# Planning the next batch's attention apart from its token mixing, with x and u in one buffer

## The chip, the cores and the metric

The kernel runs on one core of a Trainium2 chip. The metric is device time in microseconds (us), the median of the runs of one kernel. The core has TensorE (PE, matrix products into PSUM, a memory of eight banks), VectorE (DVE), ScalarE (ACT), GpSimd (POOL), which here mostly issues loads, and SyncE (SP), which here issues transposes and stores. 16 DMA engines carry out what POOL, SP and ACT issue.

## The reference, cut to what matters

Eight batches of sliding-window attention (8 heads of 64, 576 positions, a window of 128, a linear distance bias), whose output x (576 x 512 per batch) goes through a mixer: token mixing across the positions, then channel mixing, each with a residual.

```
scores = scale * q @ k.T;  masked to 0 <= rel < 128, plus -slope*|rel|
x      = softmax(scores) @ v                      # heads side by side: 576 x 512
h      = relu(x.T @ w_tok1) @ w_tok2              # 576 -> 256 -> 576
u      = x + h.T
out    = u + relu(u @ w_ch1) @ w_ch2              # 512 -> 1536 -> 512
```

## The kernel before, in words

The whole program is straight-line code. `Plan` collects operations (`op`, `dma`), each with an engine, a cost, the buffers it makes, adds to, rewrites or reads, and a **rank**. `Plan.run` then simulates the engines with those costs and at each step starts, on the engine that is free first, the ready operation of the lowest rank; `Plan.emit` writes the instructions in the order so found. On the chip each engine runs its own list strictly in that order, with semaphores for the waits. So costs and ranks only shape the order; a due time that has been given to an operation (`after`) does too, and is no wait on the chip. `NUDGES` is a list of `number:rank shift:due time` for single operations, by their number in the order of creation.

A `Ring` is a set of equal buffers; `plan.buf(name)` takes the first that comes free. `x` of two batches (a pair, 2 x 576 rows as nine blocks of 128, the ninth, `TAIL`, holding 64 rows of each) lies in ring `xb`, which has one buffer, and `u` in ring `ub`, which has two. q and k blocks go through five `qk` slots, v blocks through five `v` slots, transposed q/k through seven `qkT` slots.

Work per batch `b`:

- **Loads**: `load` issues q, k, v of each block on POOL, in one fixed order (pair by pair, blocks 0, 1, 2, 3, 7, TAIL, 4, 5, 6, and in each q, k, v), each waiting for a free slot. A **hold** is a small POOL copy that reads batch `b`'s finished uT at a set place in this order, so everything behind it on POOL waits until that uT is complete. Before, `HOLDS = {4: ("v", 3, 0)}`: ahead of v of pair 3, block 0, POOL waits for batch 4's uT.
- **Attention** (`side`): `transposes` (from pair 1 on by SP's DMA transpose, line 761), `scores` (line 809: products over 64 rows into PSUM banks 0 to 3, `TWO`; line 824: two exponentials on ACT; line 834: masks on DVE), `scores_two` (line 855, two blocks of two pairs at once), `values` (line 897: products with v into one of the four single banks 4 to 7; lines 910, 913 and 919: reciprocal and normalisation into x).
- **Token mixing** (`token_mix`): line 944 x with `W1`, line 954 the tail rows, relu, line 987 with `W2`, line 1005 u = x + product on DVE; then u is transposed into uT, for batches 0 to 2 on PE (line 1022), from batch 3 on by SP's DMA transpose (line 1013).
- **Channel mixing** (`main`): first product by `chunk` (line 1502) or, where `UNITS` says so, by `unit` (line 1402, fewer products and more sums); second product by `second` (line 1679); line 1545 and 1590 for the tail; results evicted on DVE (lines 1650, 1597) and stored.

While `main(b)` runs, `side(b + 1)` is planned beside it, so that PE always has channel products to run between the steps of the attention. What decides their order is the rank. `along(base, length, total)` gives ranks that rise from `base` to `base + length` as the costs add up to `total`. `main(b)` rises over its own length `n`; before, `side(b + 1)`, attention and token mixing in one sequence, rises over `SPREAD * n`, with `SPREAD = 0.38`:

```
side(nb, along(base - 1e5, 1.0, 1.0) if b == 0 else along(base, SPREAD * n, tot))
```

Of the kernel before, what the change touches and what calls it, by code (L numbers as in the profile page):

```python
# [14 lines left out]


SEM = 40.0
SPREAD = 0.38


class Buf:
# [10 lines left out]
    def __call__(self):  # L32
        got = self.ring.slots[self.slot[0]]
        return got if len(self.slot) == 1 else self.ring.pair(self.slot)


class Ring:
# [34 lines left out]
class Plan:  # L72
# [9 lines left out]
    def op(self, eng, cost, emit, rank, makes=(), adds=(), rewrites=(), part=None, uses=(), reads=(), needs=(),  # L82
           after=0.0, order=None, bus=0.0, other=None, mode=0, behind=(), narrow=False):
        def many(x):
            return list(x) if isinstance(x, (list, tuple)) else [x]

        o = Op()
        o.eng, o.cost, o.emit, o.rank, o.after, o.part = eng, cost, emit, rank, after, self.part
        o.t0 = o.done = None
        o.order, o.bus, o.other, o.mode, o.narrow = order, bus, other, mode, narrow  # L90
        o.n = len(self.ops)
        o.deps = set(many(needs))
        o.behind = list(behind)
        o.bufs = []
        for b in many(makes):
            b.writers.append(o)
            o.bufs.append(b)
        for b in many(adds):
            o.deps.update(b.writers)
            b.writers.append(o)  # L100
            o.bufs.append(b)
        for b in many(rewrites):
            o.deps.update(u for u in b.users if u not in b.later)
            b.later.append(o)
            b.writers.append(o)
            o.bufs.append(b)
        if part is not None:
            b, key = part
            b.parts.setdefault(key, []).append(o)
            o.bufs.append(b)  # L110
        for b in many(uses):
            o.deps.update(b.writers)
            o.bufs.append(b)
        for b, key in many(reads):
            o.deps.update(b.parts[key])
            o.bufs.append(b)
        o.deps.discard(o)
        for b in o.bufs:
            b.users.append(o)
        self.ops.append(o)  # L120
        return o
# [204 lines left out]
    def emit(self, spin):  # L326
# [20 lines left out]
        for _, _, go in sorted(work, key=lambda w: w[:2]):  # L347
# [15 lines left out]
FROM_U = 3  # L363
# [22 lines left out]
GROUPS = (((0, 1, 2, 3), 250),)  # L386
UORDER = (1, 5, 2, 6, 3, 7, 4)
UNIT_RANK = 0
NUDGES = ("611:-21079:100923 615:-377:0 618:6245:106227 624:11583:0 628:-3532:0 631:-20512:118175 632:4405:0 "
          "635:13739:113529 638:-6964:114135 641:43614:0 643:-19605:120680 648:13951:125840 652:20901:132489 "  # L390
          "656:1592:130617 662:-3783:94988 668:12595:102360 672:0:99525 676:-4021:0 691:3986:0 694:4455:102094 "
          "706:-16795:109525 710:11799:0 717:5009:114541 723:-30772:115527 725:-13156:0 727:1700:0 731:-799:113884 "
          "737:-15688:124087 742:88:126037 747:-10649:132061 750:-29110.6:133561.55 752:1864:0 753:7662:141715 "
          "756:18322:0 757:13696:0 758:5979:130815 759:2748:0 760:-6228:0 761:25117:132703 763:-2147:0 765:-1777:134943 "
          "766:12861:138150 769:4570:135329 774:-3476:0 778:14785:0 780:7181:136913 782:6347:136777 796:5332:0 799:9009:0 "
          "801:8201:142134 808:2736:0 813:9918:154475 818:-1109:0 820:-5330:154387 833:-4650:0 835:34387:124325 "
          "837:-15506:120235 843:8673:0 857:-16826:126349 858:1715:130121 859:24976:132690 862:8001:133653 "
          "869:22770:125235 870:11407:127731 885:3734:139098 891:9282:135579 895:-4722:0 906:6597:0 929:-1024:0 "
          "934:1522:0 937:4392:0 939:-1560:0 942:20915:0 948:771:175554 950:-4529:179605 951:995:176861 980:-2682:165866 "
          "981:-2735:0 983:1098:0 989:-8428:0 992:-4728:0 995:4194:0 1000:4211:156722 1005:3799:169472 1010:-2057:164371 "  # L400
          "1013:-4825:0 1019:7261:0 1032:-2615:175960 1038:-4243:0 1044:-3493:182549 1047:-1700:185338 1048:8146:185482 "
          "1054:3724:185348 1056:2724:0 1068:-1298:0 1070:3393:0 1074:20899:194114 1077:45251:0 1080:18007:0 "
          "1081:-2386:195024 1087:458:209375 1088:1:199812 1091:-1643:199488 1097:-2044:205608 1111:2214:211061 "
          "1114:17600:0 1119:-16086:212462 1121:-6088:0 1124:52293:0 1133:0:215904 1147:208:186538 1149:1234:0 "
          "1154:3339:0 1163:6504:0 1166:5025:0 1173:-13218:195991 1174:-7990:194582 1175:11221:198039 1181:18370:199015 "
          "1189:-770:198395 1195:5140:0 1201:243:206584 1202:-5634:204124 1213:15048:0 1219:1629:209744 "
          "1232:-23729:221022 1233:-4369:0 1235:2272:0 1237:-12249:0 1238:-11167:221075 1240:4249:0 1241:4209:0 "
          "1242:7504:0 1255:5295:0 1256:0:234956 1257:14642:0 1258:12581:0 1260:3619:0 1262:4895:0 1264:11531:232963 "
          "1267:-4292:227279 1276:5714:238024 1280:962:0 1283:-2021:240378 1288:-141:235787 1290:-9906:246722 "
          "1305:-17082:0 1316:331:0 1318:-36744:224142 1320:-20516:0 1325:23513:0 1328:7362:0 1331:-20168:227572 "  # L410
          "1332:-6676:0 1335:2767:0 1338:-7764:230640 1343:-4826:0 1344:8492:0 1347:6686:0 1361:914:0 1363:6921:0 "
          "1364:10157:0 1367:6998:238996 1368:-7883:243068 1371:-1965:238074 1378:-1479:249284 1382:8303:0 1386:7721:0 "
          "1399:-2853:246581 1401:-6638:250221 1402:-752:252012 1403:-9427:251897 1407:-2824:0 1427:-5105:253889 "
          "1431:-2423:252435 1443:3256:263701 1444:354:262085 1457:-151:263359 ")
UNIT_LATE = False
SECOND_LATE = False
GATE = True
BANKS = 8
ALIKE = 0
PAUSE = 150  # L420
HOLDS = {4: ("v", 3, 0)}
UNITS = [0, 0, 0, 3, 0, 3, 2, 3]
FILL = 60000.0
START = 4300.0
# [27 lines left out]
def kernel(  # L452
# [59 lines left out]
    ring("qkT", QT, [P, 2 * NHP, P])  # L512
    ring("pe", 3, [P, 2, 4, 2, P])
    ring("rt", 4, [P, 2, 4, 1], F32)
    ring("xb", 1, [P, NB, DM])
    ring("ub", 2, [P, NB, DM])
    ring("xt", XT, [P, DM])
    ring("r10", 1, [P, NJ, DM])
    ring("r11", 1, [P, NJ, DM])
# [518 lines left out]

    def opening(rank):

        xb, ub = xbs[0], ubs[0] = plan.buf("xb"), plan.buf("ub")
        r1 = r1s[0] = plan.buf("r10")
        uT = plan.buf("uT")
        uts[0] = (uT, None, list(range(NC)))
# [265 lines left out]
            mix(hp)  # L1310
        wides.append(marks["first"])

    def side(b, rank):
        pr, half = b // 2, b % 2
        if half == 0:
            xbs[pr], ubs[pr] = plan.buf("xb"), plan.buf("ub")
        two = pr in PAIRED
        if half:
            units = [5, 6, 7] + [TAIL] * (pr == 0) + [NC] if two else [4, 5, 6, 7] + [TAIL] * (pr == 0)
        else:  # L1320
            units = [1, 2, 3, TAIL] if pr - 1 in PAIRED else [0, 1, 2, 3, TAIL]
            if pr - 1 in PAIRED:
                values(pr, 0, None, marks["next"], rank, 0)
        prev = None
        for u in units + [None]:
            if u is not None:
                need = [(pr, u)]
                if half and u == 5:
                    need.insert(0, (pr, NC))
                if u == TAIL and pr:  # L1330
                    need.append((pr, 2 * NC - 1))
                if half and u == NC and two:
                    need.append((pr + 1, 0))
                for w in need:
                    if w not in qkT or (u == TAIL and w[1] == TAIL and pr == 0):
                        transposes(*w, rank(0 if by_transfer(*w) else 450))
                hf = half if u == TAIL and pr == 0 else None
                if half and u == NC and two:
                    pb = marks["next"] = scores_two(pr, rank(450))
                else:  # L1340
                    pb = scores(pr, u, hf, rank(450), wides if b == 1 else ())
            if prev is not None:
                values(pr, prev[0], prev[1], prev[2], rank)
            prev = None if u is None else (u, hf, pb)
        token_mix(b, rank)

    def gated(*bufs):
        for x in bufs:
# [368 lines left out]
    for b in range(B):  # L1717
# [5 lines left out]
        if b + 1 < B:  # L1723
            nb = b + 1
            tot = SIDE[min(nb // 2, 1)][nb % 2] + 8 * 216 + 216 + (5 if nb % 2 else 4) * (656 if nb < FROM_U else 432)
            if nb > 1:
                tot -= 450 * sum(by_transfer(nb // 2, x) for x in (ORDER[:6], ORDER[6:])[nb % 2])
            side(nb, along(base - 1e5, 1.0, 1.0) if b == 0 else along(base, SPREAD * n, tot))
            for o in wait:
                o.behind.append(marks["score"])  # L1730
            for x in gates:
                x[0] = marks["score"]
# [39 lines left out]
```

## Time and profile before

| | |
|---|---|
| median of 3 runs | 274.07 us (273.73 to 274.9) |
| span of the profiled execution | 272.2 us |
| median less that span | 1.87 us |
| PE busy | 263.6 us, 97% |
| weight loads busy | 191.8 us, 70% |
| DVE, ACT, POOL busy | 224.7, 150.7, 114.7 us |
| loads' DMA queue | 89.4% of 16 engines' span |
| instructions | 7391 |

The page gives the profiled execution's time as its span, from the first to the last instruction; the runs' times also hold what lies around the span. Rows of the views name the line, the engine, the operation and `out<-in` by the program's tile names, with x and a count; in brackets or behind a bar stands the idle time ahead of an instruction and what ended it.

### The profile page before, as it was taken

Reading aid. Unit: us, or ns where it says so; the run is one execution under the profiler, and the core shown is the slowest. Engines: PE = TensorE matmul, PEld = TensorE weight load, DVE = VectorE, ACT = ScalarE, POOL = GpSimd, SP = SyncE. Lnnn points to the kernel's source line nnn. Section 1 sums busy time; section 2 is a strip of 40 time slices with the busy share of each in tenths; the row PEclk is TensorE's granted clock in tenths of the full one; section 3 lists DMA queues with packets and bytes.
Section 4 is the critical chain, followed back from the end, with each engine's and each line's share of the span. In section 5 each row is a group of like instructions: output and inputs, shape, how many; then the busy total and the mean of one; then the engine's idle time right before and its main releaser. Section 6 shows DMA issues by size and latency. Waiting matters only on the chain.

```text
span 272.2 us, 7391 instructions
## 1 busy us (share of the span) xinstructions
PE 263.6 (97%) x2965; PEld 191.8 (70%) x2992; DVE 224.7 (83%) x520; ACT 150.7 (55%) x267; POOL 114.7 (42%) x147
## 2 busy tenths in 40 slices
PE   7989999999999999999999999999999999999994
PEld 5767566676686655587786756498886758589883
DVE  7887699978897569688999478698998989976983
ACT  6973796226881298107992089308973089506700
POOL 8978796840397007800870307800651050004000
PEclk9999999999999999999999999999999999999999
DMA  8999999999999979999999999999999580035005
GB/s 201 178 173 180 167 148 183 157 156 175 186 127 161 192 162 78 137 119 210 200 149 119 142 228 96 140 154 142 212 132 67 110 239 2 2 82 171 4 10 183
DMA packets 160338, 38.59 MB, mean 142 GB/s; under 512 B 146544, under 2 KB 159472, under 8 KB 160304
## 3 DMA queue, kind: packets, MB, share of 16 engines
q0 software_dynamic: 109968, 19.64, 89.4%
q1 hardware_dynamic: 49104, 17.70, 33.4%
q10 hardware_dynamic: 1232, 0.79, 1.0%
q8 instruction: 23, 0.38, 0.5%
q14 instruction: 11, 0.09, 0.1%
HBM read 35.85 MB, written 9.44 MB: 166 GB/s over the span
## 4 chain that ended last, share of the span: by engine, by line
PE 90%; DMA 3%; POOL 3%; issue 1%; ACT 1%; DVE 0%; POOLq 0%
PE ps L1679 27%; PE ps L1502 15%; PE ps L1402 12%; PE ps L897 6%; PE ps L809 5%; PE ps L987 4%; PE ps L944 4%; PE ps L1545 4%; PE ps L1590 4%; DMA W<-in_moe_w_tok_dram 2%; POOL v L623 1%; DMA qkT<-qk 1%; POOL qk L630 1%; PE ps L772 1%; PE ps L1488 1%
## 5 line engine op out<-in xcount | busy, mean ns | idle before, releaser
L614 POOL DMA_DIRECT2D v<-in_v_dram x36 | 30.5, 849 | 76.4 <-PE ps L897 72.8
L824 ACT ACTIVATE pe<-ps 128x1024 bf16<-128x1024 f32 (+1 forms) x56 | 51.3, 969 | 3.1 <-PE ps L809 3.0
L1502 PE MATMUL ps<-uT,WC 128*128 128x512 bf16 x182 | 46.0, 379 | 0.7 <-issue 0.2
L1508 ACT ACTIVATE r<-ps 128x512 bf16<-128x512 f32 x45 | 26.4, 601 | 35.9 <-PE ps L1502 33.8
L1679 PEld LDWEIGHTS <-r 128*128 128x128 bf16 x384 | 36.8, 98 | 7.4 <-issue 0.7
L1679 PEld LDWEIGHTS <-s 128*128 128x128 bf16 x288 | 27.8, 98 | 5.8 <-DVE s L1527 0.4
L614 POOL DMA_DIRECT2D qk<-in_k_dram x35 | 30.3, 873 | 3.7 <-DMA qk<-in_k_dram 1.6
L834 DVE TENSOR_TENSOR pe<-pe,mask 128x1024 bf16<-128x1024 bf16 (+1 forms) x48 | 30.5, 650 | 1.6 <-ACT pe L824 1.4
L614 POOL DMA_DIRECT2D qk<-in_q_dram x35 | 30.2, 867 | 3.7 <-DMA qkT<-qk 1.7
L1502 PEld LDWEIGHTS <-WC 128*128 128x128 bf16 x196 | 17.7, 98 | 18.1 <-issue 0.5
L1417 ACT COPY raw<-ps 128x512 f32<-128x512 f32 x27 | 15.5, 597 | 22.6 <-PE ps L1402 22.6
L1679 PE MATMUL ps<-WC,r 128*128 128x256 bf16 x192 | 24.9, 273 | 0.0
L1679 PE MATMUL ps<-WT,s 128*128 128x256 bf16 x192 | 24.7, 273 | 0.0
L1679 PE MATMUL ps<-WT,r 128*128 128x256 bf16 x192 | 23.8, 273 | 0.1
L897 PEld LDWEIGHTS <-pe 128*128 128x128 bf16 (+1 forms) x480 | 19.5, 99 | 5.6 <-DVE pe L834 0.8
L1426 DVE TENSOR_TENSOR r<-ps,raw 128x512 bf16<-128x512 f32 x30 | 20.2, 680 | 3.3 <-ACT raw L1417 2.8
L897 PE MATMUL ps<-v,pe 128*128 128x65 bf16 (+1 forms) x480 | 22.8, 194 | 0.1
L1005 DVE TENSOR_TENSOR ub<-ps,xb 128x512 bf16<-128x512 f32 x32 | 20.5, 683 | 2.7 <-ACT r L1508 0.9
L913 DVE TENSOR_TENSOR xb<-ps,rt 128x256 bf16<-128x256 f32 (+1 forms) x52 | 21.4, 417 | 0.5
L1650 DVE TENSOR_TENSOR raw<-ps,ub 128x512 f32<-128x512 f32 x25 | 17.0, 686 | 5.8 <-PE ps L1679 5.8
L1402 PE MATMUL ps<-tt,WS 128*128 128x256 bf16 x132 | 18.8, 273 | 0.1
L809 PEld LDWEIGHTS <-qkT 64*128 64x128 bf16 x448 | 11.9, 94 | 8.3 <-issue 5.9
(143 smaller groups left out, 479.4 us busy)
## 6 DMA issues: line engine op xcount, KB each, us to landing
out_dram<-raw SPq DMA_DIRECT2D x19, 256.0 KB, 4.4
qk<-in_q_dram POOLq DMA_DIRECT2D x30, 128.0 KB, 5.4
qk<-in_k_dram POOLq DMA_DIRECT2D x30, 128.0 KB, 5.4
v<-in_v_dram POOLq DMA_DIRECT2D x28, 128.0 KB, 5.1
WC<-in_moe_w_ch_dram POOLq DMA_DIRECT2D x8, 384.0 KB, 7.5
out_dram<-raw POOLq DMA_DIRECT2D x6, 256.0 KB, 3.4
out_dram<-ob SPq DMA_DIRECT2D x5, 256.0 KB, 4.1
v<-in_v_dram POOLq DMA_DIRECT2D x16, 64.0 KB, 4.8
```

The lines of the kernel that those rows point to most:

```text
L614: nc.gpsimd.dma_start(out=to()[p0 : p0 + n, :, :], in_=rows(src, b, s0, n))
L809: pe_.matmul(wide(e)[:, i, kind, a:z], lhsT=ts[kb]()[e * D : (e + 1) * D, NHP + i, :], rhs=ts[blk]()[e * D : (e + 1) * D, i, a:z], start=T ...
L824: act_.activation(out=pb()[:, e, :, lo:, c0:c1_], in_=wide(e)[:, :, lo:, c0:c1_], func=ACT.Exp, scale=scale)
L834: dve_.tensor_tensor(out=o, in0=o, in1=heads(mk, es), op=ALU.mult)
L897: pe_.matmul(view()[a:z, at, i, :], lhsT=pb()[:, e, i, kind, a:z], rhs=vb()[:, h, 0 : D + 1], start=m == 0, stop=m == len(mms) - 1, skip_g ...
L913: dve_.tensor_tensor(out=x4(), in0=view()[r0:r1_, :, :, 0:D], in1=rt()[r0:r1_, 0:n, :, :].broadcast_to([r1_ - r0, n, 4, D]), op=ALU.mult)
L1005: plan.op("DVE", 690, lambda blk=blk, ht=ht, hs=hs: dve_.tensor_tensor(out=ub()[:, blk, :], in0=ht()[:, hs], in1=xb()[:, blk, :], op=ALU.a ...
L1402: pe_.matmul(bk()[:, c * HS : (c + 1) * HS], lhsT=l(c, cb), rhs=r(cb), start=new and c == 0 and cb == 0, stop=cb == 1, skip_group_check=True)
L1426: add = plan.op("DVE", 690, lambda: dve_.tensor_tensor(out=o(), in0=half_of(bk), in1=half_of(e), op=ALU.add), rk + UNIT_RANK, uses=[bk, e] ...
L1502: pe_.matmul(ct()[:, :], lhsT=WC1[:, cb, t * P : (t + 1) * P], rhs=uT()[:, cb, :], start=cb == 0, stop=cb == NCB - 1)
L1508: plan.op("ACT", 600, lambda t=t, ct=ct: act_.activation(out=r2()[:, t, :], in_=ct()[:, :], func=ACT.Relu), rk, part=(r2, t), uses=[ct], o ...
L1679: pe_.matmul(bk()[:, c * HN : (c + 1) * HN], lhsT=l(t, c), rhs=w(t), start=first, stop=g == 1 and t == HK - 1, skip_group_check=True)
```

## The change

- Ring `xb` (one buffer) and ring `ub` (two) become one ring `xu` of three. A pair takes one buffer; u is written over x. `View` gives u its own list of writers and parts on x's buffer.
- `side` takes two ranks: one for attention, one for token mixing. Attention's ranks of batch `b + 1` go from `base - 0.2 n` to `base + 0.2 n`, those of its token mixing from `base + 0.2 n` to `base + 0.35 n`. For batch 1 both stay as they were.
- The holds become `{2: ("k", 2, 0), 4: ("k", 3, 8)}`: a new one ahead of k of pair 2, block 0, waits for batch 2's uT; that for batch 4 moves from ahead of v of pair 3, block 0, to ahead of k of pair 3, block 8 (TAIL).
- Another list of `NUDGES`: 145 entries in place of 178. It reaches back to operation 155; that of before begins at 611.

```diff
-SPREAD = 0.38
+SCORE = (-0.2, 0.4)
+TOKEN = (0.2, 0.15)
...
+class View:
+    def __init__(self, buf):
+        self.buf, self.writers, self.parts, self.later = buf, [], {}, []
+
+    def __call__(self):
+        return self.buf()
...
-            o.bufs.append(b)
+            o.bufs.append(getattr(b, "buf", b))
...
-NUDGES = ("611:-21079:100923 615:-377:0 618:6245:106227 624:11583:0 628:-3532:0 631:-20512:118175 632:4405:0 "
...
+NUDGES = ("155:0:56492 156:63405:0 160:24808:0 297:-72622:0 300:0:37910 316:0:47700 323:0:46277 326:0:53492 "
...
-HOLDS = {4: ("v", 3, 0)}
+HOLDS = {2: ("k", 2, 0), 4: ("k", 3, 8)}
...
-    ring("xb", 1, [P, NB, DM])
-    ring("ub", 2, [P, NB, DM])
+    ring("xu", 3, [P, NB, DM])
...
-        xb, ub = xbs[0], ubs[0] = plan.buf("xb"), plan.buf("ub")
+        xb = xbs[0] = plan.buf("xu")
+        ub = ubs[0] = View(xb)
...
-    def side(b, rank):
+    def side(b, rank, rank2):
         pr, half = b // 2, b % 2
         if half == 0:
-            xbs[pr], ubs[pr] = plan.buf("xb"), plan.buf("ub")
+            xbs[pr] = plan.buf("xu")
+            ubs[pr] = View(xbs[pr])
...
-        token_mix(b, rank)
+        token_mix(b, rank2)
...
-            side(nb, along(base - 1e5, 1.0, 1.0) if b == 0 else along(base, SPREAD * n, tot))
+            mixt = 8 * 216 + 216 + (5 if nb % 2 else 4) * (656 if nb < FROM_U else 432)
+            if b == 0:
+                near = along(base - 1e5, 1.0, 1.0)
+                side(nb, near, near)
+            else:
+                side(nb, along(base + SCORE[0] * n, SCORE[1] * n, tot - mixt), along(base + TOKEN[0] * n, TOKEN[1] * n, mixt))
```

More of the change, by code (lines that the diff above doesn't have):

```diff
@@ L100, in op @@
             b.writers.append(o)
-            o.bufs.append(b)
+            o.bufs.append(getattr(b, "buf", b))
         for b in many(rewrites):
@@ L105, in op @@
             b.writers.append(o)
-            o.bufs.append(b)
+            o.bufs.append(getattr(b, "buf", b))
         if part is not None:
@@ L109, in op @@
             b.parts.setdefault(key, []).append(o)
-            o.bufs.append(b)
+            o.bufs.append(getattr(b, "buf", b))
         for b in many(uses):
             o.deps.update(b.writers)
-            o.bufs.append(b)
+            o.bufs.append(getattr(b, "buf", b))
         for b, key in many(reads):
             o.deps.update(b.parts[key])
-            o.bufs.append(b)
+            o.bufs.append(getattr(b, "buf", b))
         o.deps.discard(o)
@@ L388 @@
 UNIT_RANK = 0
-NUDGES = ("611:-21079:100923 615:-377:0 618:6245:106227 624:11583:0 628:-3532:0 631:-20512:118175 632:4405:0 "
[L390 to L414, printed above, removed]
```

19 rows, old and new, of the table NUDGES are left out of this document.

## The prediction

> **What bounds the kernel now.** I read the page first (span, busy shares, chain), then the busy time by stretch, what TensorE waited for, and the timelines around the places that the change touches.
>
> ```profile
> span 272.2 us, 7391 instructions
> PE 263.6 (97%) x2965; PEld 191.8 (70%) x2992; DVE 224.7 (83%) x520; ACT 150.7 (55%) x267; POOL 114.7 (42%) x147
> PE 90%; DMA 3%; POOL 3%; issue 1%; ACT 1%; DVE 0%; POOLq 0%
> ```
>
> TensorE (PE) is busy 263.6 of 272.2 us and makes 90% of the chain that ended last. Everything else only matters where it makes PE wait. The next view tells where PE is idle; its columns are the stretch, its length, and busy us with instruction counts for PE, weight loads, VectorE, ScalarE, GpSimd, then the granted clock.
>
> ```profile
> 0.00:20.00 20.00, 17.30 (x295) 12.95 (x295) 16.38 (x60) 15.15 (x29) 17.55 (x28) 1.00 1.44 184
> 20.00:120.00 100.00, 99.06 (x1070) 65.63 (x1083) 81.76 (x185) 54.46 (x92) 55.75 (x68) 1.00 1.69 158
> 120.00:140.00 20.00, 19.38 (x280) 16.14 (x281) 18.36 (x46) 15.56 (x27) 8.40 (x10) 1.00 1.29 175
> 140.00:160.00 20.00, 19.74 (x170) 13.89 (x174) 15.02 (x29) 7.29 (x15) 5.44 (x7) 1.00 1.26 146
> 160.00:260.00 100.00, 99.58 (x1086) 75.82 (x1092) 86.72 (x193) 58.20 (x107) 27.56 (x35) 1.00 0.86 114
> 260.00:268.53 8.53, 8.53 (x79) 7.39 (x76) 6.02 (x11) 0.00 (x0) 0.00 (x0) 1.00 0.32 103
> 268.53:272.20 3.67, 0.00 (x0) 0.00 (x0) 0.42 (x1) 0.00 (x0) 0.00 (x0) 1.00 0.40 119
> ```
>
> Idle PE time is 2.70 us in the first 20, 3.67 us behind the last matmul (an eviction and a store), and 0.94 + 0.62 + 0.26 + 0.42 = 2.24 us in between. The clock is 1.00 throughout. The opening and the last store are not touched, so what an order can win in plain sight is 2.24 us, 0.8% of the time.
>
> The view hides some idle time, because a matmul's end is modelled: its record overlaps the next.
>
> ```profile
> 124.52 0.23 PE L809 MATMUL ps<-qkT 64*128 64x128 bf16 x2 [0.42 <-DMA qkT<-qk]
> 127.28 0.60 PE L1402 MATMUL ps<-tt,WS 128*128 128x256 bf16 x4
> 127.82 0.23 PE L809 MATMUL ps<-qkT 64*128 64x128 bf16 x2
> 129.31 0.60 PE L1402 MATMUL ps<-tt,WC 128*128 128x256 bf16 x4
> 129.74 0.60 PE L1402 MATMUL ps<-uT,WC 128*128 128x256 bf16 x4
> L824 ACT ACTIVATE pe<-ps 128x1024 bf16<-128x1024 f32 (+1 forms) x56 | 51.3, 969 | 3.1 <-PE ps L809 3.0
> ```
>
> Four product matmuls last 0.60 us by their record but the next four follow after 0.43 (129.31 to 129.74), so a wait of up to 0.17 us is unseen. Ahead of a score stage, which uses 64 rows, the step is 0.54 (127.28 to 127.82): 0.11 us go into the change of shape. There are 28 score stages (56 exponentials, two each); entering and leaving makes 56 changes. The change keeps their number: two score stages can't be neighbours, since each takes all of PSUM banks 0 to 3. What may hide in waits at them is at most 56 x (0.17 - 0.11) = 3.4 us. So the bound on the whole gain is taken as 2.24 + 3.4 = 5.6 us.
>
> **x and u in one buffer.** No instruction comes or goes: u is added into x's place, each element read and written by the same VectorE operation. What goes is a wait: with one x buffer, the next pair's first normalised block has to wait for the last read of this pair's x.
>
> ```profile
> 109.05 0.28 PE L897 MATMUL ps<-v,pe 128*128 128x65 bf16 x4
> 116.50 1.29 DVE L1005 TENSOR_TENSOR ub<-ps,xb 128x512 bf16<-128x512 f32 x2
> 121.02 0.42 DVE L913 TENSOR_TENSOR xb<-ps,rt 128x256 bf16<-128x256 f32 x1
> 180.17 0.41 PE L897 MATMUL ps<-v,pe 128*128 128x65 bf16 x8
> 181.63 0.42 DVE L913 TENSOR_TENSOR xb<-ps,rt 128x256 bf16<-128x256 f32 x1
> ```
>
> At pair 2 the values are multiplied at 109.05, but their normalisation into x comes at 121.02, after the last u addition that reads the old x (116.50 + 1.29 = 117.79). One of four single PSUM banks is held for 12 us. At pair 3 the first normalisation follows after 1.46 us (180.17 to 181.63), so this wait is worth something at one boundary. Next in line there is qkT: PE's one named wait in mid-program is the 0.42 us at 124.52. I book 120 to 160, the stretch behind this boundary, as won: 0.62 + 0.26 = 0.88 us; between nothing and 0.88.
>
> **Attention ahead of mixing.** Before, scores and mixing of the next batch share 0.38 of a batch; by the code's own costs (4650 of 8322 for an even batch) scores take its first 0.21, mixing 0.21 to 0.38. After, scores spread from -0.2 to 0.2, mixing from 0.2 to 0.35. So mixing stays, and attention gets twice the room, starting a fifth of a batch sooner. What this relieves is ScalarE:
>
> ```profile
> 190.00:200.00 10.00, 10.00 (x175) 8.74 (x176) 9.46 (x22) 10.00 (x18) 5.76 (x7) 1.00 1.44 183
> 220.00:230.00 10.00, 9.95 (x145) 7.76 (x144) 9.62 (x26) 9.72 (x16) 1.18 (x3) 1.00 0.37 111
> ```
>
> ScalarE is full (10.00, 9.72 of 10) while attention runs, yet PE is busy 10.00 and 9.95 there, because channel products cover it. So I book little: half of the 0.94 us of 20 to 120, 0.47, and none of the 0.42 behind 160; bounds 0 and 1.36. Of the unseen 3.4 us I book a sixth, 0.55, nearer to none, since the visible waits at the same places are small too; bounds 0 and 3.4.
>
> **The holds.** GpSimd issues all q, k and v loads in order; a hold makes everything behind it wait until the u of one batch is transposed.
>
> ```profile
> POOL v L614 <- PE ps L897: 72.8, 12, 15.7
> 83.16 0.93 POOL L614 DMA_DIRECT2D qk<-in_k_dram  x1
> 90.86 0.61 PE L1022 MATMUL ps<-ident,ub 128*128 128x128 bf16 x8
> 102.38 0.88 POOL L614 DMA_DIRECT2D v<-in_v_dram  x1 [15.68 <-PE ps L897]
> 153.90 0.18 POOL L1036 COPY zero<-uT 1x4 bf16<-1x4 bf16 x1 [10.94 <-DMA uT<-ub]
> 164.17 0.88 POOL L614 DMA_DIRECT2D v<-in_v_dram  x1 [7.13 <-PE ps L897]
> qk<-in_k_dram POOLq DMA_DIRECT2D x30, 128.0 KB, 5.4
> ```
>
> The new hold for batch 2 costs one 0.18 us copy and moves four loads (k, v, q, k, the first at 83.16) behind batch 2's last u transpose at 90.86 plus its copy, about 92. They then land by some 92 + 4 x 0.93 + 5.4 = 101, and the next load waited until 102.38 anyway, for a v slot that attention frees. Booked at nothing; the cover is about 1.3 us, and a load that outlasts it is late by so much. Who waits for these loads is SP's transpose of that block and, behind it, batch 3's double score stage (line 855). The old hold for batch 4 moves 14 loads further on: v, q, k of pair 3 (154.41 on before) may go at 143 beside batch 4's u transposes; what follows waits for v slots as before (164.17).
>
> ```profile
> L1013 SPq DMA_TRANSPOSE uT<-ub x4: 1190/1224/2043, 115.1 to 119.1; - x4
> DMA to landing us min/median/max: 3.1/3.6/4.0
> L1013 SPq DMA_TRANSPOSE uT<-ub x4: 1190/1206/1217, 145.5 to 149.4; - x4
> DMA to landing us min/median/max: 2.3/2.4/4.3
> L761 SPq DMA_TRANSPOSE qkT<-qk x5: 1231/1262/1279, 121.3 to 127.5; - x5
> DMA to landing us min/median/max: 3.1/3.3/3.3
> L761 SPq DMA_TRANSPOSE qkT<-qk x5: 1232/1524/2806, 71.8 to 91.2; - x5
> DMA to landing us min/median/max: 3.7/7.1/8.9
> ```
>
> Beside loads u's transposes land in 3.6 instead of 2.4 us: 1.2 us late, covered by the attention that now stands there; 0 booked, 1.2 if that cover is gone. The q/k transposes land in 7.1 instead of 3.3 us. The Trainium skill (DMA: Bandwidth & Descriptors, Queues, rings and completion order) says that a DMA engine takes turns between the queues that have work, packet by packet. By that rule alone an overlapped transpose would take twice its time, an estimate of 6.6 us; the trace has 7.1 and the measurement is used.
>
> **The sum.** 0.88 + 0.47 + 0.55 = 1.9 us. The profiled span is 272.2; the median of the runs is 274.07, so 1.87 us lie around the span and stay. 272.2 - 1.9 + 1.87 = 272.2 us, 0.7% faster.
>
> **Rivals.** *The idle time only moves* (0.16): PE was busy 9.95 of 10 or more where attention filled ScalarE, and the five v slots (72.8 us of GpSimd's waiting is for PE to free one) may not let attention run ahead at all, so that the change doesn't do what it says. Then only some 0.4 us of the boundary are won: 273.7.
>
> *Scores stand ahead of their transposes* (0.27, slower). PE runs in its written order. Attention a fifth of a batch sooner puts the q/k transposes among loads, where they land 7.1 - 3.3 = 3.8 us later. It decides where a score stage stands less than 3.8 us behind its planned landing: PE then waits, and with it all channel products written behind it. One such place costs the gain and more: 274.07 - 1.9 + 3.8 = 276.0; two give 279.8. For it: PE's one named wait in mid-program (0.42 us at 124.52) is of this kind. Against it: it is the only one in seven batches, although q/k transposes were slow (7.1) from 71.8 to 91.2 too.
>
> *More idle time than shows* (0.10): all 2.24 us and half of the unseen 3.4 go: 274.07 - 3.9 = 270.1. The Trainium skill (Perfetto Trace Analysis, Identifying the Most-Contended Engine) holds that matmul busy time is a poor measure of the distance to the roofline and the weight loads' busy share a better one. By it, room would be 272.2 - 191.8 = 80.4 us, an estimate of no use here.
>
> ```profile
> L1502 PE MATMUL ps<-uT,WC 128*128 128x512 bf16 x182 | 46.0, 379 | 0.7 <-issue 0.2
> L1502 PEld LDWEIGHTS <-WC 128*128 128x128 bf16 x196 | 17.7, 98 | 18.1 <-issue 0.5
> ```
>
> On line 1502 weights load for 17.7 us while PE streams for 46.0 with 0.7 us idle, so a free weight port is no free PE.
>
> **How the numbers follow.** The forecast has 0.47, the rivals 0.16, 0.27 and 0.10. A difference under 0.5% (1.4 us) can't be told from none here. Faster by over 0.5% is the forecast and the third rival, 0.57; within it the first, 0.16; slower the second, 0.27. The forecast's own range is 271.3 to 272.7. The whole range runs from the third rival's 270.1 to 277.5, between one late score stage and two; outside lie about half of the third rival and a third of the second, 0.14.
>
> **What would show it.** Right: PE idle in 120 to 160 under 0.3 us; the first normalisation of pair 2 within 2 us of its products; a second small copy from uT on GpSimd near 92; score stages of a batch spread over more time, and no ScalarE stretch of 10 us at 10.00. Wrong: waits of PE for qkT over 1 us each, q/k transposes landing in over 7 us behind 100 us, or PE's busy time (263.6) changed by more than 2 us, which would say that the work under the order isn't the same.

## The result and the profile after

The changed kernel takes 278.55 us (median of 15 runs, 275.42 to 280.51) against 274.13 us (15 runs, 273.73 to 277.15). The ratio is 1.0108 with an interval of 1.0074 to 1.0142: slower by 3.0 us (2.0 to 3.9), where 272.2 us, 0.7% faster, was forecast. (The ratio leaves out five runs of the changed kernel that lie over 1.5% above its fastest, two of them at a clock of 1.000; the medians do not, and differ by 4.4 us. Below, us are worked out from ratios, times 274.1.)

The page of the changed kernel, its span, engines and chain:

```profile
span 278.7 us, 7392 instructions
PE 265.7 (95%) x2963; PEld 193.8 (70%) x2991; DVE 230.1 (83%) x528; ACT 147.0 (53%) x253; POOL 114.8 (41%) x148
PE 77%; DVE 9%; DMA 9%; issue 2%; ACT 1%; SPq 0%; DVEq 0%; ACTq 0%
```

This execution had a granted clock of 0.986, so part of its 2.1 us more of busy PE is clock. The same kernel was profiled again at a clock of 1.000, and the readings below are from that profile:

```profile
span 277.7 us, 7392 instructions
PE 263.7 (95%) x2963; PEld 191.7 (69%) x2991; DVE 229.8 (83%) x528; ACT 146.9 (53%) x253; POOL 114.7 (41%) x148
PE 70%; DMA 13%; DVE 10%; issue 3%; POOL 2%; ACT 1%; DVEq 0%; POOLq 0%; ACTq 0%
```

PE is busy 263.7 us, as before (263.6), and idle 14.0 instead of 8.6. The work has not changed; all the 5.4 us are waits, and on the chain PE's 90% has become 70%, with DMAs at 13% and VectorE at 10%. The busy time by stretch of that profile (columns as in the prediction) says where:

```profile
0.00:20.00 20.00, 17.14 (x295) 12.79 (x296) 16.35 (x60) 15.27 (x29) 17.59 (x28) 1.00 1.40 180
20.00:120.00 100.00, 98.53 (x1060) 65.05 (x1075) 82.32 (x185) 54.82 (x92) 55.85 (x69) 1.00 1.70 159
120.00:140.00 20.00, 18.71 (x282) 16.20 (x281) 17.36 (x43) 13.41 (x19) 5.04 (x7) 1.00 0.88 148
140.00:160.00 20.00, 19.61 (x165) 13.65 (x169) 16.27 (x33) 7.78 (x18) 8.60 (x10) 1.00 1.80 158
160.00:260.00 100.00, 95.76 (x1042) 71.68 (x1051) 85.08 (x186) 54.62 (x96) 26.91 (x35) 1.00 0.86 114
```

Idle PE was 0.94, 0.62, 0.26 and 0.42 us in the last four of these stretches; it is 1.47, 1.29, 0.39 and 4.24. The waits of PE name three places (us in all, times, longest):

```profile
PE ps L1406 <- ACT raw L1421: 2.1, 1, 2.1
PE ps L1406 <- DVE tt L1369: 1.3, 1, 1.3
PE ps L1683 <- DVE raw L1654: 1.3, 1, 1.3
```

Together 4.7 of the 5.4 us, and none of the three is in the profile of before. The timeline of the same profile around each (start, length, engine, line, in brackets the idle time ahead and what ended it):

```profile
118.94 0.29 PE L899 MATMUL ps<-v,pe 128*128 128x65 bf16 x4
120.07 0.41 DVE L915 TENSOR_TENSOR xu<-ps,rt 128x256 bf16<-128x256 f32 x1
...
122.50 0.43 DVE L1369 TENSOR_TENSOR tt<-uT 128x512 bf16<-128x512 bf16 x1 [2.02 <-DMA uT<-xu]
122.84 0.68 DVE L1654 TENSOR_TENSOR raw<-ps,raw 128x512 f32<-128x512 f32 x1
123.58 1.47 PE L1683 MATMUL ps<-WT,r 128*128 128x256 bf16 x12 [1.29 <-DVE raw L1654]
...
185.06 7.87 SPq L763 DMA_TRANSPOSE qkT<-qk  x5
193.03 1.61 SPq L1666 DMA_DIRECT2D out_dram<-raw  x3
196.34 0.58 ACT L1421 COPY raw<-ps 128x512 f32<-128x512 f32 x1 [2.07 <-DMA out_dram<-raw]
196.97 0.60 PE L1406 MATMUL ps<-tt,WS 128*128 128x256 bf16 x4 [2.05 <-ACT raw L1421]
...
251.51 0.43 DVE L1369 TENSOR_TENSOR tt<-uT 128x512 bf16<-128x512 bf16 x1 [2.75 <-DMA uT<-xu]
251.99 0.60 PE L1406 MATMUL ps<-tt,WS 128*128 128x256 bf16 x4 [1.32 <-DVE tt L1369]
```

- *122.50, the eviction.* VectorE runs its list in order. The difference of two uT blocks of batch 3 (line 1369) stands ahead of an eviction (line 1654) and waits 2.02 us for a transpose. The eviction, whose products had ended by 121.9, waits with it, and PE waits for the bank.
- *196.34, the output buffer.* Three stores were queued on SP behind five q/k transposes that took 7.87 us to issue. ScalarE needs the buffer that the first store empties.
- *251.51, the last u transpose of batch 7.* PE has nothing else to run until its difference is there.

The u transposes of batch 4, and all the q/k transposes from 99.5 us on, in that profile (issues, then us from issue to landing):

```profile
L1015 SPq DMA_TRANSPOSE uT<-xu x4: 1193/1228/1636, 149.0 to 154.7; - x4
DMA to landing us min/median/max: 2.4/4.3/5.6
L763 SPq DMA_TRANSPOSE qkT<-qk x18: 1231/1250/2210, 99.5 to 220.1; - x18
DMA to landing us min/median/max: 3.2/3.4/5.2
```

### The profile page after: what moved, and what is told of

The parts are those of the page before. It is cut to its first block, busy times and chain, and to the rows that moved or that the text cites. A ratio compares the mean times of both kernels' runs of the same rounds, so it can differ in the third digit from the quotient of the medians.

```text
span 278.7 us, 7392 instructions
## 1 busy us (share of the span) xinstructions
PE 265.7 (95%) x2963; PEld 193.8 (70%) x2991; DVE 230.1 (83%) x528; ACT 147.0 (53%) x253; POOL 114.8 (41%) x148
## 4 chain that ended last, share of the span: by engine, by line
PE 77%; DVE 9%; DMA 9%; issue 2%; ACT 1%; SPq 0%; DVEq 0%; ACTq 0%
PE ps L1683 21%; PE ps L1506 15%; PE ps L1406 10%; PE ps L899 6%; PE ps L811 5%; PE ps L946 4%; PE ps L1594 3%; PE ps L989 3%; DMA uT<-xu 3%; DMA qkT<-qk 3%; PE ps L1549 3%; DVE xu L1007 2%; DMA raw<-in_q_dram 2%; DMA out_dram<-raw 1%; DVE r L1430 1%
## 5 line engine op out<-in xcount | busy, mean ns | idle before, releaser
L899 PE MATMUL ps<-v,pe 128*128 128x65 bf16 (+1 forms) x480 | 23.6, 196 | 0.1
L899 PEld LDWEIGHTS <-pe 128*128 128x128 bf16 (+1 forms) x480 | 20.1, 100 | 5.1 <-DVE pe L836 0.8
L1666 POOL DMA_DIRECT2D out_dram<-raw x6 | 4.3, 719 | 45.3 <-ACT r2t L1554 21.4
L915 DVE TENSOR_TENSOR xu<-ps,rt 128x256 bf16<-128x256 f32 (+1 forms) x54 | 22.1, 416 | 0.5
L1007 DVE TENSOR_TENSOR xu<-ps,xu 128x512 bf16<-128x512 f32 x32 | 20.8, 682 | 1.0 <-PE ps L989 0.9
L1406 PEld LDWEIGHTS <-WS 128*128 128x128 bf16 x176 | 16.0, 97 | 5.7 <-issue 2.8
```

What stands on the lines that cost most here:

```text
L899: pe_.matmul(view()[a:z, at, i, :], lhsT=pb()[:, e, i, kind, a:z], rhs=vb()[:, h, 0 : D + 1], start=m == 0, stop=m == len(mms) - 1, skip_g ...
L915: dve_.tensor_tensor(out=x4(), in0=view()[r0:r1_, :, :, 0:D], in1=rt()[r0:r1_, 0:n, :, :].broadcast_to([r1_ - r0, n, 4, D]), op=ALU.mult)
L1007: plan.op("DVE", 690, lambda blk=blk, ht=ht, hs=hs: dve_.tensor_tensor(out=ub()[:, blk, :], in0=ht()[:, hs], in1=xb()[:, blk, :], op=ALU.a ...
L1406: pe_.matmul(bk()[:, c * HS : (c + 1) * HS], lhsT=l(c, cb), rhs=r(cb), start=new and c == 0 and cb == 0, stop=cb == 1, skip_group_check=True)
```

## The experiments

All ratios are to the kernel before, run beside them on the same chip.

| kernel | median us | ratio | interval |
|---|---|---|---|
| after, again | 278.74 | 1.0115 | 1.0072 to 1.0158 |
| before's order, shared buffer | 274.35 | 0.9999 | 0.9981 to 1.0018 |
| after, no holds | 282.70 | 1.0255 | 1.0211 to 1.0300 |
| after, nine output buffers ("E2") | 277.05 | 1.0097 | 1.0063 to 1.0132 |
| E2, old hold | 281.40 | 1.0242 | 1.0181 to 1.0303 |
| E2, stores held back | 278.35 | 1.0120 | 1.0072 to 1.0169 |
| E2, difference later ("E7") | 276.63 | 1.0073 | 1.0034 to 1.0112 |
| E2, all three | 279.19 | 1.0155 | 1.0100 to 1.0211 |
| E7, hold behind v ("E12") | 275.58 | 1.0046 | 1.0022 to 1.0070 |
| after, packets shifted | 277.30 | 1.0111 | 1.0077 to 1.0144 |
| before, packets shifted | 275.04 | 1.0033 | 1.0002 to 1.0063 |
| E7, packets shifted | 278.84 | 1.0142 | 1.0098 to 1.0186 |
| no list: old ranks, old holds | 278.85 | 1.0132 | 1.0109 to 1.0154 |
| the same, again | 278.97 | 1.0172 | 1.0139 to 1.0205 |
| no list: new ranks, old holds | 278.42 | 1.0133 | 1.0106 to 1.0161 |
| no list: old ranks, new holds | 278.93 | 1.0146 | 1.0129 to 1.0164 |
| no list: new ranks, new holds | 277.66 | 1.0100 | 1.0082 to 1.0117 |
| the same, nine buffers, hold behind v | 278.57 | 1.0129 | 1.0087 to 1.0170 |

**The shared buffer alone.** The kernel after, unchanged, ran beside these as their yardstick. First the one part that can be done by itself, in before's order:

> The changed kernel once more, as the base of the other three and for a second profile. Theory A (the order counts on DMA landings that come later on the chip; PE, in order, waits behind them): 275.5 to 278.5 us, and the profile shows PE idle again near 124 (u of batch 3 landing) and near 195 to 198 (an output buffer not yet stored). Theory B (x and u in one buffer cost time of their own): the same time, but the lost time spread over the u additions and normalisations. Theory C (the holds let loads run beside u's transposes): the same time, lost where transposes land late, near 118, 152 and 184. If the 1.6 us that the profiled execution lost in its first 30 us are chance, this profile doesn't have them.

```diff
-    ring("xb", 1, [P, NB, DM])
-    ring("ub", 2, [P, NB, DM])
+    xus = [sb.tile([P, NB, DM], BF16, name=f"xu{i}") for i in range(3)]
+    plan.ring("xb", xus[0:1]); plan.ring("ub", xus[0:2])
...                # once the order is fixed: x and u of pair p both in slot p % 3
```

> The kernel before, in its own order on every engine, with x and u in one buffer: that part of the change alone. Theory B: at least 1.4 us slower than before, 275.5 or more. Theories A and C: within 0.3% of before (273.5 to 274.9), and no first normalisation of a pair waits for the old x, though VectorE's order may leave it late.

0.9999: in this order the buffer costs nothing and brings nothing. VectorE's list still puts pair 2's first normalisation 12.0 us behind its products (110.34 to 122.32), so the run doesn't show what the wait for x was worth.

**More output buffers.** Room comes from the third `xu` buffer; the order stays.

```diff
-    ring("xu", 3, [P, NB, DM])
+    ring("xu", 2, [P, NB, DM])
...
-    plan.ring("ob", raws + [sb.tile([P, DM], F32, name=f"ob{i}") for i in range(5 - 2 * RAW)])
+    outs = raws + [sb.tile([P, DM], F32, name=f"ob{i}") for i in range(9 - 1 - 2 * RAW)]; plan.ring("ob", outs[0:6])
...                # once the order is fixed: each result takes the one of the nine that is free longest
```

> The same order, but nine output buffers in turn instead of six (x and u in two shared buffers instead of three, which the order doesn't feel). Theory A: ScalarE's copy at 197 no longer waits for a store, PE's 2.1 us wait behind it is gone, and the time is 2 to 3 us under the changed kernel beside it. Theories B and C: no change, within 1 us of it.

The 2.1 us wait on line 1421 is gone. The waits of PE in this kernel:

```profile
PE ps L857 <- DMA qkT<-qk: 1.3, 1, 1.3
PE ps L1683 <- DVE raw L1654: 1.1, 1, 1.1
```

The median fell by 1.7 us beside the kernel after (278.74 to 277.05), though the ratios' intervals overlap: another wait, 1.3 us for the first q/k transposes of pair 3, has partly taken its place.

**No holds.** Neither small copy is written out.

```diff
-            plan.op("POOL", PAUSE, lambda: nc.gpsimd.tensor_copy(out=zero[...], in_=uT()[...]),
+            plan.op("POOL", PAUSE, lambda: None,
```

> The changed kernel's order with neither hold written out: loads go as soon as their slots are free. Theory C in the form that the later hold does harm by letting loads run beside batch 4's u transposes: no gain here, since they run beside them too; in the form that waiting at a hold makes loads late: 1 us or more faster than the changed kernel. Theory A: within 1 us of the changed kernel, since the two late landings that cost most (near 118 and 190) are not behind a hold.

The waits of PE (one row), and the landing of the three q/k transposes of 86 to 105 us:

```profile
PE ps L811 <- DMA qkT<-qk: 2.9, 2, 2.0
L763 SPq DMA_TRANSPOSE qkT<-qk x3: 1237/2468/3264, 88.2 to 96.6; - x3
DMA to landing us min/median/max: 7.4/8.7/9.5
```

Without holds 1.0255 instead of 1.0115, 3.8 us more (2.9 between the profiled spans, both at a clock of 1.000), and the wait for qkT that the second rival spoke of is there. The four loads that the hold for batch 2 puts off (94.8 to 97.4 us in the kernel after) go at 86.6 to 90.2 here, beside those transposes, so that hold is what keeps the wait away; taking it out alone was not tried.

**The old hold.** On E2, the hold for batch 4 stands ahead of v of pair 3, block 0, again.

```diff
+    hold.t0 = ...                     # between k and v of pair 3, block 0, and all behind it later
```

> On the base of nine output buffers: GpSimd's hold for batch 4 stands at its old place again, ahead of v of pair 3, block 0; every other list is the same. Theory A says that a landing counts only where PE's order stands close behind it: the transposes of batch 4's u and of pair 3's first block land in under 4 us (4.3 to 5.0 without), PE's wait at the double score stage near 156 (1.3 us in the last profile) goes to under 0.3, and the time falls by 0.5 to 1.2 us against nine output buffers alone (277.1). Against it: the wait stays, and then the transposes are late for another reason than the three loads at 146 to 150.

The u transposes land in 2.4 us in the median, but:

```profile
PE ps L899 <- DMA v<-in_v_dram: 3.3, 1, 3.3
```

4.0 us slower than E2 (1.0242 to 1.0097), but part of that is clock: its four runs had 0.988 to 0.994, E2's 0.997 to 1.000, and PE is busy 268.2 us in its profile against 265.8 in that of the third kernel below, which has the old hold too, at 0.999. That one, with the old hold and the store hold on E7, is 2.2 us slower than E7. So the old hold costs this order 2 to 4 us. PE comes to v at about 160 and gets it at 163.3, since the hold lets its load go at 157.2 only: in this order the hold had to move because attention moved.

**Stores held back; the difference later; all three.** On E2: POOL's last stores of batch 6 wait for batch 7's uT (first); batch 3's first difference moves behind two evictions on VectorE (second); both and the old hold (third).

```diff
+    first.emit = held                 # a small copy from batch 7's uT ahead of those stores
...
+    first.t0 = dve[dve.index(first) + 2].t0 + 1.0
```

> On the same base: one more hold on GpSimd, ahead of batch 6's first store, that waits for batch 7's uT. Theory A: the last u transpose of batch 7 lands in 2.4 us instead of 4.5 to 4.9, PE's wait near 250 (0.9 to 1.3 us behind the difference of uT on VectorE) is gone, and the time falls by 1 to 1.5 us against 277.1. Against it: the landing stays late, so it isn't the stores; or PE waits for an output buffer instead.

> On the same base: on VectorE, batch 3's first difference of uT goes behind two evictions that it stood ahead of. Theory A: the difference still waits for the late landing near 122, but PE's wait of 1.0 to 1.3 us for the eviction is gone, and the time falls by 0.7 to 1.3 us against 277.1. Against it: PE meets the landing itself at the next product and waits as long there.

> All three together with nine output buffers. Theory A: the gains add, 277.1 - 0.8 - 1.2 - 1.0 = 274.1, the kernel before's time, and PE idles over 0.3 us at none of the four places. If the order had further waits of the kind that only come up once these are gone, 275 to 276.

The store hold missed: the last u transpose still lands in 4.2 us, with no load or store in flight, but with an instruction packet (see below) at 246.0, so the stores are not what delays it. The later difference worked as far as it reaches. PE in 100 to 140 and 140 to 160 of that kernel; the kernel after has 38.55 us of the first 40 in its second profile, and 0.16 of the difference are product records that this profile has and that one lacks (see the account of the prediction):

```profile
100.00:140.00 40.00, 40.00 (x490) 1.00 1.33 143
140.00:160.00 20.00, 19.01 (x160) 1.00 1.72 166
```

The eviction's wait is gone, and 1.0 us now stands at the next place, in 140 to 160. The three together lose by the old hold: PE waits 3.5 us for v.

**The instruction packets.** In all traces a 16 KB packet comes on the queue named "instruction" about once in 256 PE instructions (23 of them, 0.38 MB). In the kernel after one falls into the last u transpose of batch 7; in that of before it comes behind it. The landing of batch 7's last u transposes, of before first and then of the kernel after, and below them that queue in the 5 us from the latter's last transpose on:

```profile
L1013 SPq DMA_TRANSPOSE uT<-ub x4: 1189/1200/1217, 237.1 to 243.6; - x4
DMA to landing us min/median/max: 2.3/2.3/2.4
L1015 SPq DMA_TRANSPOSE uT<-xu x4: 1205/1214/1217, 242.6 to 246.5; - x4
DMA to landing us min/median/max: 2.3/2.3/4.9
q8 instruction: 1, 0.02, 1.5%
```

To move the packets, 112 semaphore increments that nobody reads were put into PE's list between 27 and 102 us, with no other change; once into the kernel after, once into before, once into E7. A fourth kernel moves the hold for batch 4 behind v of pair 3, block 0, which the old hold had delayed, on E7 (E12).

```diff
+                               ...); count()      # pe_.sem_inc(mark), for the first 112 products
```

> The kernel after, same work and same order, with 112 more instructions in TensorE's list: a semaphore increment that nobody reads behind each of the first 112 channel products of batch 0. Instruction packets of 16 KB come once in some 256 TensorE instructions; so from 45 us on each of them comes some 112 instructions earlier than in the kernel after, and those at 119, 152, 178, 191 and 250 us no longer meet the last u transposes of batches 3, 4, 5 and 7 (by the traces' own rows they would come near 101, 130, 161, 187, 246). Theory F (the packet delays the transposes, and the new order has no slack behind them): the u transposes of 143 to 156 land in at most 4.5 instead of 5.7 us, the last of batch 7 in 2.3 to 3.0 instead of 3.9 to 4.9; the steps at 120, 155 and 250 us (0.9 to 1.9 us each) shrink by 2 to 3 us in all: 275.5 to 276.8 us, ratio 1.005 to 1.009. Rival O (the order itself has no slack, whatever the packets do; loads make the transposes late): landing as before, 278 to 279 us, ratio 1.010 to 1.016. If the increments themselves cost, both kernels with them show it.

> The kernel before with the same 112 increments: the control. The increments stand behind products of 512 columns, so they should cost nothing by themselves. By the traces' rows the packets then come near 127, 160, 184, 201, 219 and 242 instead of 119, 151, 177, 189 and 246. Theory F: the late transposes move from batch 3, 4 and 5 to others, and the order has slack behind them: 273.5 to 274.8 us, ratio 0.998 to 1.003. Rival O: the same, 274. A cost of the increments by themselves (112 x 17 ns = 1.9 us) would give 276.

> The kernel after with nine output buffers and batch 3's first difference behind two evictions (the run before with these two parts: 276.6 us, 1.0073), and the 112 increments. Theory F: the late transposes of batch 4 and of batch 7 go, 1.5 to 2.5 us: 274.0 to 275.2 us, ratio 0.999 to 1.004, no slower than the kernel before. Rival O: 276.6 us, 1.007.

> The same base with nine output buffers and the later difference, no increments; GpSimd's hold for batch 4 stands behind v of pair 3's first block, ahead of q of its second block, and not ahead of k of block 8. So q and k of block 1 and all behind it go after batch 4's u is transposed, near 153 us, while v of block 0 still goes near 146. Theory L (loads beside the u transposes of 143 to 156 make the step at 155): they land in 2.4 to 3.5 us instead of 4.4 in the median, and the 1.0 to 1.3 us at 155 go: 275.4 us, ratio 1.004. Rival F: the packet at 151 us makes most of it, the largest landing stays over 4 us and the time at 276.6 (1.007). If q and k of block 1 come too late, TensorE waits for qkT by 2 to 4 us and the time is 278 to 280.

The control loses 0.9 us (1.0033), of which 0.7 in its profile is a new wait of PE for uT that a moved packet meets, so the increments themselves cost little. The kernel after stays where it was (1.0111); set against the control it may have gained those 0.9 us, which is within the intervals. E7 gets slower (1.0142; by the profiled spans, 275.2 to 274.9, hardly), and not 1.5 to 2.5 us faster, as theory F expected. The packets now meet other transposes: batch 7's median rises from 2.3 to 3.4 us, while PE waits 1.7 us for qkT. Moving them brings neither kernel to before, so where they fall is at most a small part of what separates the two, and batch 4's u transposes are late without them too. Their landing in the shifted kernel, where no packet came between 146 and 161, and in E12:

```profile
L1015 SPq DMA_TRANSPOSE uT<-xu x4: 1202/1218/1233, 147.4 to 153.3; - x4
DMA to landing us min/median/max: 2.3/3.5/5.4
L1015 SPq DMA_TRANSPOSE uT<-xu x4: 1189/1216/1226, 147.6 to 153.6; - x4
DMA to landing us min/median/max: 2.3/3.1/4.4
```

So there the loads count, as theory L said: with two loads fewer beside them the median is 3.1 instead of E7's 4.9 us, and PE is busy 19.75 of 20 us in 140 to 160. E12 is at 1.0046, the nearest to before of all that have the new order.

**The list of single shifts.** What is left of the change are the new ranks and the new list. The list can be left out: `NUDGES = ""`, with old or new ranks and old or new holds, the shared buffer in all four.

```diff
-NUDGES = ("155:0:56492 156:63405:0 ...
+NUDGES = ""
...                                     # old ranks:
-                side(nb, along(base + SCORE[0] * n, ...), along(base + TOKEN[0] * n, ...))
+                one = along(base, 0.38 * n, tot); side(nb, one, one)
```

> The kernel after with an empty list of single shifts (NUDGES), the old ranks (one sequence over 0.38 of a batch) and the old hold (batch 4 ahead of v of pair 3, block 0). The corner that the other three are compared with. Nothing hand-set is left but the holds; 275 to 280 us.

> Empty list, new ranks (attention from -0.2 to 0.2, mixing from 0.2 to 0.35), old hold. Theory P (the forecast's step: attention ahead of mixing is worth 1.0 us by itself): 1 us under the corner with old ranks and old hold, unless v of pair 3 comes late. Theory T (attention ahead needs loads and transposes sooner than they land): slower than that corner by 2 to 4 us, with a wait of TensorE for v near 156 as in the run with the old hold (3.3 us).

> Empty list, old ranks, new holds (batch 2 ahead of k of pair 2, block 0; batch 4 ahead of k of pair 3, block 8). Theory P booked nothing for the holds: the same as the corner within 0.5 us. Theory T: the holds serve the new ranks; with the old ones the loads beside batch 4's u transposes cost 0.5 to 1.5 us.

> Empty list, new ranks, new holds: the kernel after without its list of single shifts. Theory P: 1.0 us under the corner with both old, and under the kernel with old ranks and new holds. Theory T: 1 to 4 us over the corner with both old, though 1 to 3 us under the kernel with new ranks and the old hold.

> The kernel after with old ranks, old hold and no list, once more, for a profile. 278.5 to 279.2 us, 1.013 to 1.016. If the old list saved idle time that a view can show, TensorE is idle 2 us or more in 160 to 260, where the kernel before has 0.42, in waits for VectorE's evictions and sums rather than for DMAs; if it saved hidden time, the waits are those of before and TensorE's records only take longer.

The corner with old ranks and holds is the kernel before without its list, but for where x and u lie: `Plan.run` gives it the same order on all five engines as the kernel before with an empty list. It has 1.0132 and, again, 1.0172. Before's list is worth 3.6 to 4.7 us. The new ranks with the new holds are 0.9 to 2.0 us faster than that corner and 1.3 us faster than the old ranks with the same holds; with the old hold they are level with the corner (theory T's 2 to 4 us of loss did not come, nor the wait for v). The new list is worth nothing that can be told: 1.0108 and 1.0115 with it, 1.0100 without.

The second run gave the profile: where before's list saved its time. PE in 180 to 220 and 220 to 260, first of before, then of the corner, and the one large wait in that stretch, for VectorE's evictions (line 1635 is line 1654 of the kernel after):

```profile
180.00:220.00 40.00, 39.84 (x457) 1.00 1.05 142
220.00:260.00 40.00, 39.90 (x432) 1.00 0.24 72
180.00:220.00 40.00, 38.31 (x443) 1.00 1.21 153
220.00:260.00 40.00, 39.04 (x410) 1.00 0.21 61
PE ps L1664 <- DVE raw L1635: 1.6, 3, 0.7
```

Idle PE in those 80 us is 2.65 us instead of 0.26, and before has no named wait there at all. That is 2.4 of the 4.6 us between the spans (276.8 and 272.2). Most of the rest is in PE's own records (266.1 against 263.6 us busy). Between 20 and 268 us the corner has twelve gaps of PE over 0.1 us and before has five; ahead of each the last record hides up to 0.17 us more, so that about 1.2 us of it, an estimate, is the unseen part of the same waits. Where the remaining 1 us sits was not settled.

**The new order without its list, mended.**

```diff
+    plan.run(); hold_behind(plan); respread(plan, outs)      # E12's hold, E2's buffers; NUDGES = ""
```

> The kernel after without its list of single shifts (277.7 us, 1.010), with nine output buffers and the hold for batch 4 behind v of pair 3's first block, as in the run that had 275.6 with the list. Theory N (the new list is worth nothing, what counts are the late places): 275.5 to 276.5 us, 1.003 to 1.008, the same as with the list. Rival (the new list is worth its 1 us or more once the late places are gone): 277 to 278 us. Under 274 only if the new ranks and the two mended places add up without loss.

1.0129, where E12, with the list and the later difference, has 1.0046; theory N falls. Without the list the mends bring nothing (1.0100 without them). With them the new list is worth some 2.3 us, the later difference among it. A reading that fits, though no run tests it alone: the list is not bad, but its gain stands on transposes and stores which come later than the order allows for.

## Why the prediction was wrong, step by step

**The step that failed is "The sum".** It set the gains against the 272.2 us of the old order and its 2.24 us of idle PE in plain sight. But three edits were priced and the fourth, another list of shifts, was not; it stood in the description of the change and got no term. The runs price it: taking before's list away costs 3.6 to 4.7 us, and the new list gives nothing back as the kernel stands. With that term the forecast's own gains, 1.9 us, become a loss of 1.7 to 2.8; measured were 3.0 (2.0 to 3.9).

**The idle time in plain sight** was smaller than 2.24 us. The nine-buffer kernel and E7 have the same list on PE, yet their pages read:

```profile
PE 263.6 (95%) x2963; PEld 191.8 (69%) x2991; DVE 229.3 (83%) x528; ACT 147.0 (53%) x253; POOL 114.8 (42%) x148
PE 266.0 (97%) x2991; PEld 192.2 (70%) x2991; DVE 229.3 (83%) x528; ACT 146.9 (53%) x253; POOL 114.7 (42%) x148
```

The first profile lacks 28 product records, all of 512 columns, and so do, by 27, before's 2965 beside 2992 weight loads. Where such a record is missing, a gap of 0.05 us is left in most cases. Between 20 and 268 us before has 28 gaps, and 23 of them are of this width: 1.2 of the 2.24 us, among them 0.63 of the 0.94 in 20 to 120 and all the 0.42 behind 160. Some 1.0 us was idle time that an order could win there. (The profiles of before and of the kernel after lack about as many, so their differences stand.)

**What bounds the kernel** was right: PE's busy time is the same, and every microsecond lost is PE waiting.

**x and u in one buffer**, booked at 0.88, is worth 0.0 in before's order (interval of half a us to either side), where the wait stays; what it is worth to the new ranks was not run by itself. In the kernel after the wait went as described: the first normalisation of pair 2 now comes 1.1 us after its products (118.94 to 120.07) and not 12. But idle PE in 120 to 160 is 1.68 us, not under 0.3. What was late next was not qkT but the eviction behind the difference; with that moved (E7) PE has no gap from 100 to 140, where before had 0.82 us.

**Attention ahead of mixing**, booked at 1.0 us: without lists the new ranks and holds together gain 0.9 to 2.0. Sign and size fit, but half of the term was time that can't be seen, 0.47 was read from 0.94 us of which 0.31 was idle, and with the old hold the new ranks gain nothing; that the size fits is in part luck. ScalarE has no full stretch left; its fullest of those from 100 to 250 us on the page of after:

```profile
130.00:140.00 10.00, 9.30 (x13) 1.00 0.99 154
```

**The holds**, booked at nothing, are worth much to this order: 3.8 us for both, 2 to 4 us for the move of the old one. Without lists the new holds are worth some 0.9 us to the new ranks and nothing to the old. The 1.2 us of late u transposes, "covered by the attention that now stands there", were 1.9 us in batch 4 (4.3 instead of 2.4), and the cover had holes: E12 gains 0.7 us over E7 by two loads less (their intervals overlap). SP's stores, which stand in one queue with the moved q/k transposes, were left out of the working; they made the largest wait, 2.1 us.

**The rivals.** The second gave 276.0 to 279.8 for one or two late score stages, and the result lies there, but not by its mechanism. PE waits for qkT at most 0.4 us, and behind 100 us the q/k transposes land in 3.4 us, 5.2 at most, under the 7 that was named. That the number fits is luck. Its mechanism is real, though: taking the holds out calls it up at once (2.9 us).

**The signs.** PE's busy time on the page is up by 2.1 us, which was to say that the work is not the same. That reading was wrong: the clock was 0.986, and at 1.000 it is 263.7. The second hold's copy came at 94.56 us, where 92 was worked out.

**Open.** What keeps E12 1.3 us above before is settled in part only: PE is idle 2.34 us in 160 to 260 (before 0.42; in both, 0.42 are missing records), of which named waits for batch 7's difference and for uT make 0.9 and 0.5. Before's list under the new ranks was not run, since its due times belong to the old order. No version beat the kernel before.

## What to carry to other kernels

Price a hand-set list of exceptions as an edit of its own: the small idle time that a profile shows is what is left after that list, and a new order starts without it. Before moving a stage forward, list what else stands in each in-order queue (an eviction behind a difference on VectorE, stores behind transposes on SP): two of the three large waits that came were there, not on the data that was moved. A hold and the order it serves change together: in the new order, taking the holds out cost 3.8 us and putting the old one back 2 to 4. Before adding up small gaps of a profile, compare its counts of products and weight loads.

## What the runs showed of the hardware

- An instruction packet of 16 KB, about one in 256 PE instructions, delays DMA transposes that it meets. With no load or store in flight a u transpose lands in 2.3 us; with such a packet and still no load or store, it took 4.2 (at 244.9 with the stores held back), 4.3 (at 149.4 in before) and 4.4 us (at 118.0 in the second profile of the kernel after). Counted over 19 of the 20 traces, 66 u transposes with a packet in the 2.3 us behind their issue landed in 4.1 us (median), the 314 others in 2.4.
- Loads delay them without any packet: in the shifted kernel batch 4's first u transpose, beside 128 KB loads, landed in 5.4 us.
- 112 semaphore increments on PE, behind products of 512 columns, each with a record of 51 ns (5.7 us in all), cost at most 0.9 us (1.0033, interval 1.0002 to 1.0063).
- The profiler drops records: two profiles of the same list on PE had 2963 and 2991 products, 263.6 and 266.0 us busy.
- The new order scatters more than the old: 275.4 to 280.5 us in 15 runs of the same kernel, against 273.7 to 277.2.
